# ScalarE's step order in a fused attention and MLP kernel, changed by single moves

## The chip, the cores and the metric

The kernel runs on one core of one Trainium2 chip. The metric is the device time of one execution in microseconds (us): the median of the runs of a kernel. A core has five engines that work side by side, each through its own list of instructions in order: TensorE (PE in the profile, with its weight loads as PEld), VectorE (DVE), ScalarE (ACT), GpSimd (POOL) and SyncE (SP). [...]

## The reference

A polynomial-sketch attention (batch 4, 4 heads, 1088 positions, head size 32, sketch size 8) feeds a wave MLP over the 128 joined channels:

```python
def phi(x):                                   # x: B,H,S,D; S1, S2: 8 x 32
    a = np.einsum('rd,bhsd->bhsr', S1, x)
    b = np.einsum('rd,bhsd->bhsr', S2, x)
    return np.einsum('bhsi,bhsj->bhsij', a, b).reshape(*x.shape[:-1], r * r)
q_p, k_p = phi(q), phi(k)
kv  = np.einsum('bhsf,bhsd->bhfd', k_p, v)
z   = np.sum(k_p, axis=2)
num = np.einsum('bhsf,bhfd->bhsd', q_p, kv)
den = np.einsum('bhsf,bhf->bhs', q_p, z)[..., None] + 1e-06
x = num / den                                  # then (B,H,S,D) -> (B, S, H*D)
theta  = x @ w_theta
zr, zi = x * np.cos(theta), x * np.sin(theta)
y = np.einsum('ts,bsd->btd', w_tok_r, zr) + np.einsum('ts,bsd->btd', w_tok_i, zi)
u = x + y
out = u + np.maximum(u @ w_ch, 0.0)
```

## The kernel before

The inputs come as 64-bit floats. Each 1088-long axis is cut into 9 chunks of 128 partitions, treated in 3 groups of 3 chunks. For each of the 4 batches the kernel makes the key features and the key-value sums (stages `kT`, `kf`, `kv`, `kvb`), the query slices (`qT`), the levels (products of queries with parts of the sums, `levels`), the denominators (`den`), the numerators (`num`), a balancing scale (`even`), and the angle stage (`theta`), which leaves x·cos and x·sin in a tile `z`. The token mixing is then done for pairs of batches by a Strassen-like scheme of products (`m10`, `m12`, `m20`, ...) of `z` with the rows of the two token matrices; sums that the products need are made by transfers that GpSimd issues and that add to their destination (`join`, L348, "accumulating transfers" below).

Everything is written down first as a list of 1147 steps, each an `Op` with its engine (P, V, A, G or S) and a function that issues its instructions. The tables at the head of the file then say how they are issued: `SEQUENCE` is the order of all steps, written out; an engine's own order is the order of its steps in it. `PLACES` deals every temporary tile to a slot of its class. `FILLS` asks for filler matmuls on TensorE: `(n, k)` puts k of them in front of step n, and a negative k puts them into the step's own PSUM tile before its own matmuls. No scheduler reorders anything behind this; the waits follow from the order and the slots. They are made for the built program on counts: an instruction waits for an engine's count of finished steps.

The steps of ScalarE that are spoken of below, by the profile's lines before the change:

- L619 and L621: unpacking of a half row pair of the token matrices that SyncE has loaded as 64-bit words into a `zs` tile. Two L619 turn the high words into floats in a `big` tile (one for each row), one L621 turns the low words into integers in another `big` tile, which VectorE or an accumulating transfer then adds.
- L795: copy of the key features from PSUM. L1036: copy of the levels from PSUM, three to a batch.
- L1141: copies of transposed numerator features from PSUM (the transposes are TensorE's L1137). L1150: copies of the numerators into `xT`.
- L1191: the sum of squares of `xT` (stage `even`). L1077: `xT` times that scale.
- L1094, L1097, L1098, L1100: the angle's rounding, its magnitude, its cosine and its sine; behind them VectorE's product at L334 (`zs<-ps,g`) writes `z`.
- L1359: two copies of a finished product sum out of PSUM into a spare tile (`hf`), which are handed on to later sums by accumulating transfers.

TensorE's product steps all pass through one helper, L354, and VectorE's two-operand steps through L334.

Of the kernel before, what the change touches and what calls it, by code (L numbers as in the profile page):

```python
# [53 lines left out]
    295, 136, 17, 67, 182, 185, 68, 69, 137, 241, 239, 18, 234, 235, 37, 183, 322, 242, 96, 237, 70, 71, 291,  # L54
    293, 296, 210, 72, 73, 74, 89, 90, 33, 159, 323, 310, 211, 212, 213, 75, 80, 187, 81, 306, 307, 186, 308,
    27, 28, 29, 175, 184, 176, 311, 22, 82, 83, 324, 220, 221, 297, 132, 133, 19, 84, 30, 177, 178, 160, 161,
    190, 346, 43, 163, 164, 243, 244, 85, 86, 214, 215, 135, 188, 101, 222, 223, 328, 309, 386, 87, 88, 102, 39,
    347, 350, 91, 92, 93, 169, 170, 240, 44, 97, 98, 103, 23, 410, 191, 45, 162, 112, 312, 113, 99, 313, 245,
    20, 246, 189, 349, 459, 104, 463, 464, 465, 466, 348, 352, 298, 455, 456, 457, 192, 193, 226, 139, 140, 194,
    325, 329, 458, 460, 461, 141, 462, 388, 105, 138, 195, 196, 197, 247, 299, 467, 468, 46, 394, 94, 100, 300,  # L60
    248, 249, 250, 469, 108, 198, 106, 227, 199, 302, 470, 326, 471, 353, 472, 200, 201, 202, 25, 387, 390, 473,
    251, 252, 253, 389, 142, 107, 110, 111, 474, 327, 254, 255, 256, 143, 144, 109, 475, 145, 146, 147, 203,
    204, 261, 413, 165, 301, 205, 206, 207, 303, 208, 338, 257, 258, 259, 171, 172, 47, 148, 149, 150, 351, 411,
    260, 395, 397, 151, 152, 209, 476, 402, 304, 477, 478, 479, 153, 480, 484, 481, 154, 155, 156, 157, 396,
    491, 412, 48, 267, 268, 492, 493, 494, 262, 269, 158, 216, 217, 265, 266, 485, 270, 173, 482, 483, 305, 495,
    124, 400, 125, 487, 488, 263, 271, 272, 486, 118, 405, 404, 499, 501, 114, 166, 179, 450, 496, 489, 273,
    274, 26, 167, 119, 120, 500, 330, 331, 24, 115, 490, 502, 503, 275, 339, 276, 116, 41, 168, 174, 180, 497,
    126, 370, 277, 332, 684, 688, 121, 122, 403, 224, 505, 689, 685, 504, 506, 392, 333, 690, 498, 398, 218,
    127, 128, 401, 283, 692, 693, 181, 694, 695, 42, 40, 686, 687, 691, 264, 696, 373, 228, 229, 282, 314, 697,
    279, 219, 316, 698, 699, 700, 701, 515, 517, 518, 434, 340, 117, 507, 509, 318, 315, 341, 399, 123, 702,  # L70
    129, 130, 362, 286, 284, 703, 525, 319, 451, 519, 520, 508, 225, 230, 231, 232, 317, 372, 704, 334, 524,
    705, 371, 285, 706, 709, 707, 510, 393, 511, 512, 526, 513, 710, 452, 516, 720, 713, 336, 557, 558, 406,
    559, 560, 335, 514, 708, 521, 342, 561, 562, 391, 632, 563, 564, 716, 453, 714, 553, 554, 555, 556, 721,
    722, 723, 354, 724, 715, 337, 717, 436, 522, 531, 711, 344, 712, 278, 345, 565, 566, 435, 357, 365, 454,
    725, 726, 718, 407, 719, 730, 732, 356, 634, 343, 527, 567, 568, 569, 408, 570, 571, 530, 572, 280, 281,
    355, 529, 528, 532, 533, 662, 748, 750, 418, 288, 573, 574, 523, 542, 727, 589, 590, 591, 592, 593, 582,
    585, 586, 583, 584, 733, 734, 320, 409, 594, 595, 587, 588, 575, 576, 577, 728, 747, 376, 426, 578, 579,
    639, 289, 608, 610, 739, 419, 735, 580, 581, 321, 817, 821, 822, 437, 741, 729, 749, 358, 818, 819, 823,
    751, 752, 753, 754, 813, 814, 815, 636, 414, 415, 416, 417, 360, 361, 611, 816, 635, 617, 359, 534, 374,
    375, 820, 364, 736, 755, 764, 763, 440, 377, 742, 731, 363, 537, 539, 756, 429, 366, 367, 738, 740, 737,  # L80
    759, 536, 428, 432, 368, 369, 422, 420, 424, 743, 744, 438, 745, 746, 757, 619, 620, 599, 596, 597, 824,
    825, 826, 633, 601, 421, 378, 541, 612, 621, 613, 602, 827, 828, 829, 830, 831, 607, 598, 603, 832, 623,
    761, 760, 433, 758, 762, 765, 766, 609, 538, 614, 615, 627, 600, 772, 771, 604, 775, 769, 427, 430, 605,
    606, 770, 626, 629, 640, 287, 833, 616, 618, 439, 381, 630, 643, 644, 834, 837, 835, 883, 441, 425, 379,
    382, 383, 442, 443, 446, 423, 380, 384, 385, 637, 645, 641, 774, 838, 431, 638, 622, 624, 625, 628, 631,
    642, 656, 768, 444, 448, 540, 928, 836, 535, 543, 839, 840, 767, 544, 773, 776, 658, 777, 657, 445, 447,
    449, 646, 647, 925, 841, 844, 842, 843, 845, 545, 651, 668, 846, 847, 789, 650, 859, 861, 848, 858, 655,
    788, 667, 654, 666, 549, 653, 862, 661, 863, 864, 865, 660, 786, 546, 669, 652, 648, 778, 659, 779, 860,
    866, 868, 870, 867, 884, 799, 878, 793, 850, 670, 797, 849, 852, 791, 853, 854, 550, 551, 871, 677, 930,
    671, 851, 672, 665, 681, 790, 1028, 680, 926, 798, 682, 1025, 805, 855, 649, 806, 856, 857, 877, 880, 1006,  # L90
    801, 809, 683, 663, 674, 872, 874, 873, 807, 869, 794, 802, 1027, 881, 876, 792, 1010, 1009, 810, 1024, 885,
    800, 808, 796, 875, 879, 882, 1007, 1012, 804, 787, 1008, 795, 803, 1011, 673, 893, 886, 907, 911, 1034,
    664, 910, 888, 1018, 1019, 811, 891, 901, 1026, 676, 1032, 890, 900, 889, 899, 1021, 1014, 1015, 812, 782,
    679, 1029, 1023, 783, 1035, 547, 927, 894, 895, 892, 896, 548, 897, 1047, 1013, 1044, 1016, 1017, 1046,
    1051, 940, 915, 902, 916, 909, 914, 1045, 903, 784, 1020, 934, 935, 1033, 917, 913, 898, 912, 1030, 904,
    918, 905, 678, 944, 675, 906, 924, 919, 1036, 780, 951, 942, 1039, 552, 1040, 1048, 1022, 1058, 945, 952,
    887, 922, 932, 1037, 950, 1049, 908, 929, 1070, 1053, 1054, 1052, 1055, 923, 1050, 1060, 1056, 1059, 936,
    937, 1057, 1061, 955, 943, 946, 1075, 1062, 1071, 1063, 941, 931, 1031, 1065, 1091, 1041, 1064, 1066, 921,
    781, 966, 785, 1092, 1093, 1094, 947, 963, 933, 1067, 938, 1095, 1096, 956, 961, 962, 1042, 1068, 1097,
# [5 lines left out]
    999, 1119, 1112, 1114, 1120, 1113, 1000, 1001, 1121, 1115, 1129, 1124, 1123, 1131, 1137, 1138, 1132, 1142,  # L105
    1139, 1140, 1141, 1144, 1143, 1145, 1146,
)
PLACES = (
    55, 59, 47, 48, 60, 2, 0, 14, 6, 7, 4, 11, 8, 21, 8, 8, 6, 24, 3, 46, 28, 3, 62, 61, 40, 45, 1, 60, 54, 47,
    61, 45, 46, 55, 48, 57, 49, 52, 51, 47, 60, 60, 41, 60, 54, 34, 60, 39, 59, 50, 35, 61, 42, 61, 45, 36, 48,  # L110
    46, 58, 51, 61, 58, 41, 61, 45, 37, 62, 44, 55, 48, 36, 61, 42, 56, 50, 38, 51, 50, 30, 9, 20, 58, 59, 43,
    53, 15, 57, 60, 19, 61, 44, 57, 36, 58, 43, 60, 35, 58, 42, 60, 34, 45, 51, 32, 10, 17, 57, 56, 42, 52, 13,
    58, 57, 60, 40, 55, 34, 55, 43, 58, 35, 57, 39, 62, 36, 31, 49, 29, 5, 12, 59, 62, 44, 52, 14, 58, 49, 48,
    53, 54, 50, 45, 55, 46, 47, 58, 49, 62, 53, 54, 46, 51, 46, 56, 50, 47, 62, 48, 54, 62, 43, 56, 58, 57, 31,
    58, 55, 61, 28, 55, 59, 56, 33, 55, 60, 56, 32, 16, 0, 18, 3, 4, 12, 2, 10, 21, 5, 19, 8, 14, 20, 11, 9, 7,
    22, 7, 24, 9, 23, 21, 23, 8, 26, 9, 23, 15, 26, 13, 23, 15, 25, 1, 24, 7, 22, 5, 26, 11, 25, 11, 26, 13, 24,
    5, 26, 13, 25, 19, 27, 60, 55, 57, 4, 47, 17, 22, 37, 38, 58, 55, 62, 34, 37, 56, 59, 56, 35, 36, 61, 60,
    59, 20, 57, 60, 38, 61, 59, 37, 57, 58, 34, 55, 58, 29, 60, 41, 55, 42, 27, 60, 60, 59, 6, 52, 6, 25, 34,
    37, 57, 59, 57, 34, 38, 59, 57, 56, 38, 37, 59, 56, 61, 11, 61, 56, 35, 39, 57, 61, 38, 42, 57, 61, 37, 40,
    59, 56, 28, 62, 61, 27, 61, 59, 58, 20, 49, 1, 24, 38, 35, 62, 56, 60, 38, 37, 61, 56, 59, 36, 38, 62, 59,  # L120
    62, 6, 56, 61, 36, 41, 57, 56, 34, 44, 57, 60, 35, 40, 60, 62, 30, 58, 39, 55, 44, 55, 60, 27, 60, 62, 59,
    15, 45, 15, 26, 23, 34, 36, 35, 61, 57, 55, 58, 13, 57, 58, 35, 43, 57, 57, 37, 44, 59, 60, 34, 40, 23, 33,
    31, 57, 56, 30, 33, 36, 38, 37, 35, 60, 55, 56, 42, 40, 59, 59, 42, 62, 44, 60, 41, 58, 40, 32, 29, 27, 13,
    58, 59, 61, 43, 40, 62, 59, 43, 58, 41, 62, 39, 62, 41, 62, 39, 62, 44, 61, 57, 55, 58, 43, 59, 39, 62, 58,
# [1578 lines left out]
```

## Time and profile before

| | |
|---|---|
| median of 3 runs | 222.46 us (221.44, 222.64, 222.46) |
| the profiled execution | 222.71 us |
| its span on the core | 220.9 us |
| TensorE's granted clock | 1.00 |
| TensorE busy | 213.4 us of the span |
| VectorE busy | 188.2 us |
| ScalarE busy | 130.9 us in 277 instructions |
| GpSimd | 80.3 us |
| moved by transfers | 48.78 MB |

The span is what the profiler sees between the first and the last instruction of the core; the execution's own time lies 1.81 us above it. Lines are those of the kernel's file, so all TensorE products stand under L354, told apart by their tiles. An idle time in brackets before a row, such as `[0.59 <-ACT hf L1359]`, is the time that the engine stood and the instruction that released it.

### The profile page before, as it was taken

The page shows a single profiled execution, that of the slowest core. Times are in us where ns is not written, and L with a number is a line of the kernel's source. Part 1 is how long each engine was busy: PE and PEld are TensorE (multiplying, and loading weights), DVE is VectorE, ACT ScalarE, POOL GpSimd, SP SyncE. Part 2 cuts the span into 40 slices and gives each one's busy share as a digit, 9 for nine tenths or more (in the row PEclk, how much of TensorE's full clock was granted, in tenths as well). Part 3 has the DMA queues.
Part 4 walks back from the last instruction along what each step waited for, and adds up shares of the span by engine and source line. Part 5 has one row for each costly group of instructions (what it writes and reads, how often), then busy time and mean ns, then how long its engine had stood idle before and what let it go on. Part 6 is the DMA issues. An engine that isn't in the chain of part 4 may idle for free.

```text
span 220.9 us, 4195 instructions
## 1 busy us (share of the span) xinstructions
PE 213.4 (97%) x1481; PEld 178.4 (81%) x1481; DVE 188.2 (85%) x449; ACT 130.9 (59%) x277; POOL 80.3 (36%) x119
## 2 busy tenths in 40 slices
PE   7999999999999999898999999999999999999993
PEld 4798988987898886767888887888788888888782
DVE  1698999999999999898999999699999966876452
ACT  3989789799999999889999721864030200000000
POOL 1159960001031141425163367891062829060000
PEclk9999999999999999999999999999999999999999
DMA  6999999999988989699999999999953979677332
GB/s 192 414 415 409 372 346 331 418 387 394 277 295 161 260 311 250 145 239 202 262 167 176 276 179 183 190 180 188 181 87 47 164 116 143 100 107 110 58 49 51
DMA packets 34969, 48.78 MB, mean 221 GB/s; under 512 B 19204, under 2 KB 22276, under 8 KB 34820
## 3 DMA queue, kind: packets, MB, share of 16 engines
q0 software_dynamic: 10368, 18.21, 47.0%
q1 hardware_dynamic: 24580, 30.30, 41.5%
q8 instruction: 12, 0.20, 0.3%
q14 instruction: 9, 0.07, 0.1%
HBM read 28.07 MB, written 2.23 MB: 137 GB/s over the span
## 4 chain that ended last, share of the span: by engine, by line
PE 62%; DVE 18%; ACT 8%; DMA 7%; issue 2%; POOL 0%; ACTq 0%; DVEq 0%; POOLq 0%
PE ps L354 57%; DMA big<-big 7%; DVE big L334 3%; DVE g L334 3%; DVE sm L341 2%; PE ps L388 2%; PE ps L1003 2%; DVE sm L334 2%; DVE hf L338 1%; ACT big L619 1%; DVE lv L334 1%; DVE big L338 1%; PE ps L1085 1%; DVE sm L338 1%; ACT big L621 1%
## 5 line engine op out<-in xcount | busy, mean ns | idle before, releaser
L354 PE MATMUL ps<-big,zs 128*128 128x288 f32 (+3 forms) x450 | 105.6, 385 | 1.2 <-ACT hf L1359 0.6
L354 PEld LDWEIGHTS ps<-big,zs 128*128 128x128 f32 x450 | 81.4, 190 | 18.0 <-ACT lv L1036 0.9
L348 POOL DMA_DIRECT2D big<-big x49 | 47.3, 1265 | 79.2 <-DVE big L338 21.6
L341 DVE SCALAR_TENSOR_TENSOR big<-ps,even,big 128x272 f32<-128x272 f32 (+3 forms) x34 | 16.0, 487 | 10.0 <-PE ps L354 9.9
L619 ACT ACTIVATE big<-zs 128x544 f32<-128x544 f32 x32 | 22.1, 710 | 2.8 <-DMA zs<-w_tok 1.5
L621 ACT ACTIVATE big<-zs 128x1088 int32<-128x1088 uint32 x16 | 19.5, 1228 | 1.9 <-DMA zs<-w_tok 1.1
L348 POOL DMA_DIRECT2D big<-g x10 | 11.9, 1326 | 11.4 <-ACT g L1560 5.9
L354 PE MATMUL ps<-mf,big 128*128 128x96 f32 x72 | 14.4, 295 | 0.1
L348 POOL DMA_DIRECT2D big<-hf x9 | 10.2, 1159 | 11.6 <-ACT hf L1359 7.8
L1328 ACT COPY g<-ps 128x128 f32<-128x128 f32 x2 | 0.5, 266 | 23.1 <-PE ps L1326 23.1
L338 DVE TENSOR_SCALAR big<-big 128x544 int32<-128x544 int32 (+1 forms) x33 | 14.0, 449 | 0.0
L354 PEld LDWEIGHTS <-hf 128*128 128x128 f16 (+1 forms) x144 | 12.1, 106 | 1.9 <-issue 0.6
L334 DVE TENSOR_TENSOR zs<-ps,g 128x768 f32<-128x768 f32 (+2 forms) x20 | 12.5, 627 | 0.9 <-ACT g L1100 0.9
L354 PE MATMUL ps<-big,big 128*128 128x128 f32 x72 | 11.6, 281 | 0.3 <-DMA big<-hf 0.3
L334 DVE TENSOR_TENSOR g<-lv 128x768 f32<-128x768 f32 x12 | 11.0, 953 | 0.9 <-PE ps L1137 0.8
L334 DVE CUSTOM_DVE_ANT_0 big<-big,big 128x1088 uint16<-128x1088 uint16 x16 | 11.5, 721 | 0.2
L354 PE MATMUL ps<-mv,hf 128*128 128x96 f16 x108 | 11.1, 206 | 0.3 <-DVE mv L909 0.2
L354 PEld LDWEIGHTS ps<-mf,big 128*128 128x128 f32 x72 | 10.9, 191 | 0.5 <-issue 0.4
L334 DVE TENSOR_TENSOR big<-big,hf 128x1152 f32<-128x1152 f32 x8 | 10.8, 1366 | 0.0
L354 PE MATMUL ps<-w,big 128*128 128x128 f32 x76 | 10.7, 278 | 0.0
L354 PEld LDWEIGHTS ps<-w,big 128*128 128x128 f32 x76 | 9.7, 192 | 0.9 <-ACT big L1150 0.6
L341 DVE SCALAR_TENSOR_TENSOR big<-ps,big 128x288 f32<-128x288 f32 (+1 forms) x15 | 6.6, 440 | 4.2 <-PE ps L354 3.9
(215 smaller groups left out, 439.0 us busy)
## 6 DMA issues: line engine op xcount, KB each, us to landing
zs<-w_tok SPq DMA_DIRECT2D x17, 1088.0 KB, 11.2
big<-big POOLq DMA_DIRECT2D x40, 272.0 KB, 5.6
big<-k_l SPq DMA_DIRECT2D x7, 576.0 KB, 6.8
big<-q_l SPq DMA_DIRECT2D x4, 576.0 KB, 8.3
big<-v_l SPq DMA_DIRECT2D x4, 576.0 KB, 6.7
big<-hf POOLq DMA_DIRECT2D x3, 576.0 KB, 9.6
big<-hf POOLq DMA_DIRECT2D x6, 272.0 KB, 8.6
big<-g POOLq DMA_DIRECT2D x10, 136.0 KB, 4.1
```

Of the source, the lines that this page charges most:

```text
L334: eng.tensor_tensor(out=o, in0=a, in1=b, op=f)
L338: (eng or V).tensor_scalar(out=o, in0=a, scalar1=s1, scalar2=s2, op0=op0, **kw)
L341: (eng or V).scalar_tensor_tensor(out=o, in0=a, scalar=s, in1=b, op0=op0, op1=op1)
L348: op("G", n * 2.55e-3, lambda: G.dma_start(dst(), src(), accum_op=ALU.add), w, r, kind=2)
L354: T.matmul(o, lhs, rhs, start=start, stop=stop, skip_group_check=True)
L388: T.matmul(nowhere() if out is None else out, idle()[:, 0:P], idle(), start=True, stop=True, skip_group_check=True)
L619: op("A", 0.19 + HT * 0.0009, lambda j=j: A.activation(dst[j](), words()[1][:, j * HT:(j + 1) * HT].bitcast(F32), AF.Prelu, scale=scale, a ...
L621: op("A", 0.22 + S * 0.0009, lambda: A.activation(stp().rearrange("p r n -> p (r n)"), words()[0].bitcast(U32), AF.Copy, scale=2.0**-29), ...
L1003: T.transpose(tr()[:, i * P:(i + 1) * P], x()[:, g * GC + i].rearrange("p h d -> p (h d)"), ident())
L1085: T.transpose(x()[:, i], xs()[:, off + i * P:off + (i + 1) * P], ident())
L1328: op("A", act(P), lambda: A.copy(ot()[:, :P], tp()), [ot], [tp])
```

## The change

Only the three tables at the head of the file differ. TensorE, VectorE, GpSimd and SyncE keep each its own order of steps: 421, 343, 84 and 51 of them. Of ScalarE's 248 steps the first eleven stay, and behind them steps are moved singly, some by one or two places, others by ten and more. All temporary tiles are dealt again to slots, so that some steps of other engines wait for other earlier users of a slot than before. `FILLS` gets one entry: one more filler matmul, in the PSUM tile of step 177, a key feature product of batch 2.

The stretch of the order that holds ScalarE's steps around 82 to 105 us, before and after, cut out of the tables:

```diff
@@ SEQUENCE
...
-    722, 723, 354, 724, 715, 337, 717, 436, 522, 531, 711, 344, 712, 278, 345, 565, 566, 435, 357, 365, 454,
-    725, 726, 718, 407, 719, 730, 732, 356, 634, 343, 527, 567, 568, 569, 408, 570, 571, 530, 572, 280, 281,
-    355, 529, 528, 532, 533, 662, 748, 750, 418, 288, 573, 574, 523, 542, 727, 589, 590, 591, 592, 593, 582,
-    585, 586, 583, 584, 733, 734, 320, 409, 594, 595, 587, 588, 575, 576, 577, 728, 747, 376, 426, 578, 579,
-    639, 289, 608, 610, 739, 419, 735, 580, 581, 321, 817, 821, 822, 437, 741, 729, 749, 358, 818, 819, 823,
-    751, 752, 753, 754, 813, 814, 815, 636, 414, 415, 416, 417, 360, 361, 611, 816, 635, 617, 359, 534, 374,
-    375, 820, 364, 736, 755, 764, 763, 440, 377, 742, 731, 363, 537, 539, 756, 429, 366, 367, 738, 740, 737,
...
+    556, 721, 722, 723, 724, 354, 715, 337, 522, 436, 531, 711, 712, 344, 278, 345, 435, 565, 566, 454, 725,
+    726, 718, 719, 407, 730, 732, 634, 343, 527, 365, 567, 727, 357, 568, 569, 408, 570, 571, 530, 572, 280,
+    281, 529, 528, 533, 532, 662, 748, 750, 355, 356, 418, 288, 573, 574, 523, 542, 589, 590, 591, 592, 593,
+    582, 585, 586, 583, 584, 733, 734, 320, 409, 594, 587, 588, 575, 576, 577, 728, 738, 376, 426, 578, 579,
+    639, 289, 595, 608, 610, 739, 580, 321, 817, 821, 822, 747, 581, 749, 735, 358, 818, 819, 823, 729, 751,
+    752, 754, 753, 813, 814, 815, 636, 414, 415, 416, 417, 360, 820, 361, 437, 611, 635, 617, 359, 534, 824,
+    420, 374, 375, 755, 764, 763, 440, 377, 741, 742, 731, 537, 539, 756, 363, 366, 736, 367, 740, 737, 759,
...
@@ PLACES
...
@@ FILLS
-    (290, 1), (64, 14),
+    (290, 1), (64, 14), (177, -1),
```

In this stretch 355 and 356 are a pair of L619 and 357 their L621; 365 and 437 are L621 of other rows, 419 an L619; 532 and 533 are the L1359 pair and 542 the TensorE product that goes on in the PSUM that they copy; 727 is the L1191 of batch 2; 732, 741 and 750 are L1094; 752, 753 and 754 are L1097, L1098 and L1100 of one group, and 755 is VectorE's product behind them; 588, 595 and 581 are L1150; 738, 747 and 729 are L1077; 816, 820 and 824 (this last earlier than in the order before) are the L1036 of batch 3; 764 is the TensorE product `m12` that needs 755. Among the other moves that the prediction speaks of, 178 is the feature copy L795 of batch 2, which goes from behind 177 to a place behind the L795 steps of batch 0, and 512 is the L1098 ahead of VectorE's 514.

116 rows, old and new, of tables (PLACES, SEQUENCE) are left out of this document.

## The prediction

> **What bounds the kernel now.** I read the page first, for the share of each engine.
>
> ```profile
> PE 213.4 (97%) x1481; PEld 178.4 (81%) x1481; DVE 188.2 (85%) x449; ACT 130.9 (59%) x277; POOL 80.3 (36%) x119
> ```
>
> TensorE (PE) is busy for 97% of the span, so a change of ScalarE's order can only pay through the idle left on TensorE, or through an engine that sets TensorE's pace. So the second view is busy time by stretches, in columns start:end, length, then PE, PEld, DVE, ACT, POOL, clock, DMA share and GB/s.
>
> ```profile
> 31.00:93.00 62.00, 60.80 (x575) 52.38 (x574) 60.73 (x131) 57.72 (x123) 9.48 (x12) 1.00 0.95 295
> 93.00:104.30 11.30, 10.73 (x94) 8.11 (x92) 9.45 (x23) 10.19 (x23) 4.74 (x6) 1.00 1.07 230
> ...
> 130.00:160.00 30.00, 30.00 (x201) 24.29 (x200) 26.87 (x61) 11.53 (x24) 15.77 (x18) 1.00 1.08 185
> ```
>
> Between 31 and 104 us TensorE, VectorE (DVE) and, to 93, the transfers are all almost full, and ScalarE (ACT) is 57.72 of 62. Only in 93 to 104.3 does VectorE drop, to 9.45 of 11.3. From 130 to 160 TensorE is busy without a gap and the transfers are full (a share over 1 counts packets that overlap). The third view, the waits of VectorE from 31 to 104.3, says what that drop is:
>
> ```profile
> DVE zs L334 <- ACT g L1100: 0.9, 1, 0.9
> DVE g L334 <- PE ps L1137: 0.8, 1, 0.8
> ```
>
> Two waits and no others. The fourth view, the chain that ended last (start, length, what), shows what stands in front of the longer one:
>
> ```profile
> 80.51 8.77 DMA big<-big
> 89.36 0.66 ACT big L619
> ...
> 92.05 7.72 DMA big<-big
> ...
> 154.61 61.76 PE ps L354 x286
> ```
>
> A transfer ends at 89.28 and frees ScalarE's row step L619; behind it stand the two copies L1359; behind these another transfer, L621, the sine L1100, VectorE's product L334, and the TensorE product that starts at 104.29. From there the chain holds TensorE's rows alone, of which the last begins at 154.61. So the time before is set by when TensorE reaches 104.29, and what is gained in front of it is kept as far as no later wait eats it.
>
> **The change part by part.** The order view shows TensorE, VectorE, GpSimd and SyncE with the same steps in the same order; ScalarE's 248 steps are moved from the twelfth on; buffers are dealt again; one filler matmul is added. The sum goes against the profiled execution, 222.71 us (span 220.9, 1.81 around it); the median of the three runs, 222.46, is 0.25 below, and I shift the result by that.
>
> *First wait, 87 to 92 us.* The timeline of ScalarE and that of TensorE, with the idle before a row in brackets (the rows from 95 on are for the step after the next):
>
> ```profile
> 84.58 2.38 ACT L621 ACTIVATE big<-zs 128x1088 int32<-128x1088 uint32 x2
> ...
> 87.52 0.57 ACT L1094 ACTIVATE g<-ps 128x384 f32<-128x384 f32 x1
> 89.36 1.30 ACT L619 ACTIVATE big<-zs 128x544 f32<-128x544 f32 x2 [1.28 <-DMA big<-big]
> 90.57 0.65 ACT L1359 COPY hf<-ps 128x288 f32<-128x288 f32 x2
> ...
> 91.49 1.17 ACT L1191 ACTIVATE big<-big 128x1152 f32<-128x1152 f32 x1
> ...
> 95.23 0.48 ACT L1150 COPY big<-ps 128x384 f32<-128x384 f32 x1 [0.16 <-PE ps L354]
> ...
> 99.85 1.22 ACT L621 ACTIVATE big<-zs 128x1088 int32<-128x1088 uint32 x1 [0.87 <-DMA big<-big]
> 100.97 0.48 ACT L1094 ACTIVATE g<-ps 128x384 f32<-128x384 f32 x1
> ...
> 106.95 0.61 ACT L1077 ACTIVATE g<-big,even 128x384 f32<-128x384 f32 x1
> ```
>
> ```profile
> 84.59 0.94 PE L354 MATMUL ps<-w,big 128*128 128x128 f32 x6
> ```
>
> ```profile
> 91.00 1.18 PE L354 MATMUL ps<-big,zs 128*128 128x288 f32 x4 [0.59 <-ACT hf L1359]
> 92.02 1.70 PE L1137 MATMUL ps<-ident,g 128*128 128x128 f32 x12
> ...
> 104.29 2.07 PE L354 MATMUL ps<-big,zs 128*128 128x288 f32 x8 [0.57 <-DVE zs L334]
> ```
>
> In the new order the two L621 of 84.58 go behind the L1094 of 87.52, the square L1191 goes between them, and the L1359 pair comes next, ahead of the two L619 that wait for the transfer. Without the L621 in front, the L1094 can start about 2 us sooner, at 85.5, when its six matmuls of 84.59 end. From its end at 86.1 come an L621 (2.38 for two rows that overlap by 0.1, so 1.13 each), the L1191 (1.07), an L621 of 1.13 and the pair (0.65): done at about 90.1 instead of 91.22. TensorE's product at 91.00 then starts when TensorE is free. By the bracket that is 0.59 earlier; but start to start a row here gives way sooner than its end says (91.00 + 1.18 = 92.18 against the next start 92.02, 0.16 overlap), so I take 0.59 + 0.16 = 0.75. [...] By the end times alone this term would be 0.59, by starts it is 0.75.
>
> *VectorE at 93.75.* Its timeline at the two waits:
>
> ```profile
> 93.75 0.96 DVE L334 TENSOR_TENSOR g<-lv 128x768 f32<-128x768 f32 x1 [0.80 <-PE ps L1137]
> ...
> 103.45 0.69 DVE L334 TENSOR_TENSOR zs<-ps,g 128x512 f32<-128x512 f32 x1 [0.89 <-ACT g L1100]
> ```
>
> It waits 0.80 for the transposes L1137, which follow that product and the L1141 copies. Both come 0.75 earlier, ScalarE because the L1191 now lies in front. The wait shrinks to 0.05, and VectorE runs 0.75 early, free for its next waited step at 103.45 - 0.89 - 0.75 = 101.8.
>
> *VectorE at 103.45.* The copy at 95.23 waits for TensorE and so starts at 94.48. Between it and VectorE's release the new order drops an L619 (half of 1.30, 0.60 after an overlap of 0.1), the L1094 of 100.97 (0.38) and the 0.87 of waiting for the transfer, and adds the L1077 of 106.95 (0.51), another L1150 (0.38) and a level copy L1036 (like an L1150 but wider; estimated at 0.45): -0.51. The sines themselves are then done two steps sooner, but in the built program VectorE's wait rests on a count that also takes in the L621 behind them, so I count to its end: 103.45 - 0.75 - 0.51 = 102.19, **-1.26**. TensorE's product at 104.29 follows by the same amount: its own idle of 0.57 + 0.16, with the 0.75, leaves room for 1.48 (0.16 again the overlap). It also needs the third L1036 copy of its levels, which the new order puts directly behind that L621, ready near 102.7, in front of 103.0.
>
> *The early steps.* Moves before 84 us can only cost, as VectorE and TensorE have nothing to gain there. One timeline row or two of ScalarE, TensorE and VectorE:
>
> ```profile
> 22.28 0.34 ACT L795 COPY big<-ps 128x192 f32<-128x192 f32 x1
> ...
> 76.55 0.62 ACT L1098 ACTIVATE g<-g,halfpi 128x384 f32<-128x384 f32 x1
> ```
>
> ```profile
> 28.00 0.44 PE L354 MATMUL ps<-mv,hf 128*128 128x96 f16 x2 [0.21 <-DVE mv L909]
> ```
>
> ```profile
> 78.04 0.95 DVE L334 TENSOR_TENSOR zs<-ps,g 128x768 f32<-128x768 f32 x1
> ```
>
> The feature copy at 22.28 goes some twelve steps back, to about 26.9, and a feature product that TensorE did ahead of 28.00 then waits about half a microsecond for it. The filler, one more matmul just before, adds about 0.3 if it is like one of the four at 91.00 (1.18). TensorE waits 0.21 at 28.00 anyway, for VectorE, so 0 to 0.6 of this can pass on; VectorE not being late at that place, I take 0. At 78.04 VectorE needs the cosine L1098 of 76.55; laid one after another with their row lengths, ScalarE's new steps end it at 77.9 instead of 77.17, so its slack falls from 0.87 to about 0.1. Estimated cost of the places where slack falls below 0.2: 0.1, range 0 to 0.4.
>
> *The transfers.* Row loads move because their tiles come free at other times (the new order moves several unpacking steps L619 and L621 by 2 to 9 us), but the queue is full to 93 us (DMA share 0.95), so I cost them at nothing; if that cover is gone, a late load costs its lateness at the L619 that reads it. Late in the kernel most accumulating transfers are released by TensorE's products, so they move with it; but at the DMA share of 1.08 from 130 to 160 they queue, and where a product starts right as its tile lands, an unmoved landing takes the gain back. I take 0.1 lost; the range is 0 to 1.0, the difference between the two long landings of the chain (8.77 and 7.72).
>
> The sum: -1.26 + 0.1 + 0.1 = -1.06; 222.71 gives 221.65, the median 222.46 gives **221.4 us**.
>
> **The rivals.** What this kernel's measurement can tell from no change is about 0.5%, 1.11 us, so faster means under 221.35 and slower over 223.57.
>
> *Larger gain.* If VectorE's step at 103.45 isn't held by the L621, or ScalarE arrives sooner, both waits go whole: 0.80 + 0.89 = 1.69, and with nothing lost later, 220.8. For it: the sines alone would be done near 99.8. Against: the count, and that the late losses must be zero.
>
> *Part of the gain.* Only the 0.75 is kept and 0.2 is lost: 221.9. The mechanism is the transfer of 92.05 to 99.77, for which the L621 of 99.85 waits. A row load issued behind the two L619 of 89.36 now goes out over a microsecond later, beside that transfer. If it pushes the landing from 99.77 to over 101.5, the L621 starts no sooner than in the sum plus 0.7. Against it: the transfer itself is issued behind the L1359 copies, which come 1.1 us earlier, so it can also land sooner. For it: the transfer of 80.51 took 8.77, longer than this one's 7.72, so landings move by a microsecond from one place to another. [...]
>
> *Slower.* ScalarE has only 4.3 us of idle in 31 to 93, and a moved step that has to wait stops all behind it. If waits at new places make it late, the first to pay is VectorE at 78.04, with its 0.1 of slack: beyond a cosine that ends at 78.0 each microsecond costs one, until the gain is gone at 79.2; from 80.4 the kernel is over 223.6. That takes 2.4 us of new waiting between 31 and 78: more than half of all its idle there, and I put it at 224.2.
>
> *The change doing nothing* would need both waits to come back at other places; it lies in the second rival.
>
> **How the numbers follow.** The forecast (0.6 to 1.5 gained) gets 0.46, with somewhat more than half, 0.26, past the bound, as the two losses are estimates that may be nil; the larger gain 0.16; part of the gain 0.20; slower 0.18. That gives faster 0.42, same 0.40, slower 0.18. The range goes from 220.4 (the larger gain, 220.8, with the runs' own scatter below it) to 223.8, which leaves out the worse part of the slower case. The forecast's own range is 221.0 to 221.9.
>
> **What would show it.** Right: ScalarE shows no wait above 0.3 for a transfer before its L1359 pair, TensorE's idle of 0.59 is gone, VectorE waits less than 0.1 where it waited 0.80, and TensorE's chain of products starts near 103.0. Wrong: new waits of VectorE or TensorE for ScalarE between 20 and 80 us, a landing for the L621 later than 101, or a wait of TensorE for a transfer between 130 and 160, each with its length.

## The result: slower by 0.84%, and the profile after

The changed kernel takes 1.0084 times the kernel before, with a 95% interval of 1.0055 to 1.0113 (11 runs each); on a second occasion, beside other kernels, 1.0095 (1.0055 to 1.0134). That is 1.9 to 2.1 us more. The forecast was 221.4 us, 1.1 us less; its range ended at 223.8, and 222.46 times 1.0084 is 224.3.

In some executions of either kernel the mean granted clock of TensorE is 0.97 (in the two that were traced, both of the changed kernel, it is 0.50 for 13.7 us from 21 or 22 us on), which the ratios here and below leave out but for one of h5's six. The profile below is of the second occasion, an execution at clock 1.00 (223.83 us, span 222.0).

Page, windows and VectorE's waits from 31 to 104.3 us, as they were shown of before:

```profile
PE 214.0 (96%) x1482; PEld 178.4 (80%) x1482; DVE 188.7 (85%) x449; ACT 131.9 (59%) x277; POOL 81.9 (37%) x119
```

```profile
31.00:93.00 62.00, 60.56 (x574) 52.22 (x571) 60.78 (x131) 57.23 (x119) 12.36 (x16) 1.00 0.94 294
93.00:104.30 11.30, 11.30 (x100) 8.79 (x99) 9.52 (x24) 10.48 (x22) 3.77 (x5) 1.00 1.06 231
130.00:160.00 30.00, 29.44 (x195) 23.32 (x194) 28.12 (x64) 12.21 (x26) 17.55 (x20) 1.00 1.07 182
```

```profile
DVE g L334 <- PE ps L1137: 1.2, 1, 1.2
DVE zs L334 <- ACT big L621: 0.3, 1, 0.3
```

VectorE's second wait has shrunk from 0.9 to 0.3 and now ends with the L621, as forecast, but the first has grown from 0.8 to 1.2 instead of vanishing. TensorE has 0.56 of idle between 130 and 160 where it had none. The chain that ended last says why:

```profile
81.00 10.53 DMA big<-big
91.53 0.14 issue
91.67 1.16 PE ps L354 x4
...
147.73 11.97 DMA big<-big
159.74 57.71 PE ps L354 x268
```

The transfer that landed at 89.28 now lands at 91.53, 10.53 us after its issue instead of 8.77. What follows it is no longer ScalarE but TensorE's product m20 itself. Much later a transfer stands in the chain again, right in front of the product m30 at 159.74. TensorE's and ScalarE's timelines of the changed kernel:

```profile
91.67 1.16 PE L354 MATMUL ps<-big,zs 128*128 128x288 f32 x4 [1.23 <-DMA big<-big]
...
158.26 1.18 PE L354 MATMUL ps<-big,zs 128*128 128x288 f32 x4 [0.26 <-DMA big<-big]
159.74 2.56 PE L354 MATMUL ps<-big,zs 128*128 128x288 f32 x10 [0.30 <-DMA big<-big]
```

```profile
85.59 0.49 ACT L1094 ACTIVATE g<-ps 128x384 f32<-128x384 f32 x1 [0.29 <-PE ps L354]
...
89.37 0.68 ACT L1359 COPY hf<-ps 128x256 f32<-128x256 f32 x2
```

The ScalarE row is as forecast: the L1094 starts at 85.59 (85.5 was said) and the L1359 pair is done at 90.05 (90.1 was said). It just didn't help: TensorE then waits 1.23 for the transfer.

### The profile page after: what moved, and what is told of

Read it like the earlier page. It is cut to its first block, busy times and chain, and to the rows that moved or that the text cites. A ratio compares the mean times of both kernels' runs of the same rounds, so it can differ in the third digit from the quotient of the medians.

```text
span 227.1 us, 4198 instructions
## 1 busy us (share of the span) xinstructions
PE 219.4 (97%) x1482; PEld 183.8 (81%) x1482; DVE 189.2 (83%) x449; ACT 132.0 (58%) x277; POOL 78.8 (35%) x119
## 4 chain that ended last, share of the span: by engine, by line
PE 58%; DMA 17%; ACT 10%; DVE 7%; issue 3%; POOL 3%; SPq 0%; POOLq 0%
PE ps L354 53%; DMA big<-big 15%; POOL big L348 3%; DMA big<-k_l 2%; ACT big L619 2%; PE ps L780 2%; ACT big L621 2%; DVE g L334 2%; DVE sm L341 1%; PE ps L1003 1%; PE ps L1137 1%; DVE sm L334 1%; PE ps L1085 1%; DVE hf L338 1%; ACT g L1141 1%
## 5 line engine op out<-in xcount | busy, mean ns | idle before, releaser
L348 POOL DMA_DIRECT2D big<-big x49 | 47.7, 1338 | 89.1 <-PE ps L780 26.6
L619 ACT ACTIVATE big<-zs 128x544 f32<-128x544 f32 x32 | 22.0, 714 | 2.8 <-DMA zs<-w_tok 2.8
L621 ACT ACTIVATE big<-zs 128x1088 int32<-128x1088 uint32 x16 | 19.7, 1232 | 0.0
L354 PE MATMUL ps<-mf,big 128*128 128x96 f32 x72 | 15.3, 309 | 0.1
L354 PEld LDWEIGHTS <-hf 128*128 128x128 f16 (+1 forms) x144 | 13.1, 114 | 1.7 <-DVE hf L338 0.8
L334 DVE TENSOR_TENSOR zs<-ps,g 128x768 f32<-128x768 f32 (+2 forms) x20 | 12.5, 627 | 0.4 <-PE ps L354 0.3
L354 PE MATMUL ps<-sbk,g 128*128 128x64 f32 x72 | 12.3, 324 | 0.1
L354 PEld LDWEIGHTS ps<-sbk,g 128*128 128x128 f32 x72 | 11.7, 244 | 0.5 <-issue 0.5
L354 PEld LDWEIGHTS ps<-mf,big 128*128 128x128 f32 x72 | 11.6, 203 | 0.4 <-issue 0.4
L334 DVE CUSTOM_DVE_ANT_0 big<-big,big 128x1088 uint16<-128x1088 uint16 x16 | 11.5, 720 | 0.2
L334 DVE TENSOR_TENSOR g<-lv 128x768 f32<-128x768 f32 x12 | 11.0, 950 | 0.6 <-PE ps L1137 0.5
L334 DVE TENSOR_TENSOR big<-big,hf 128x1152 f32<-128x1152 f32 x8 | 10.8, 1366 | 0.0
```

The source lines that it names most:

```text
L334: eng.tensor_tensor(out=o, in0=a, in1=b, op=f)
L348: op("G", n * 2.55e-3, lambda: G.dma_start(dst(), src(), accum_op=ALU.add), w, r, kind=2)
L354: T.matmul(o, lhs, rhs, start=start, stop=stop, skip_group_check=True)
L619: op("A", 0.19 + HT * 0.0009, lambda j=j: A.activation(dst[j](), words()[1][:, j * HT:(j + 1) * HT].bitcast(F32), AF.Prelu, scale=scale, a ...
L621: op("A", 0.22 + S * 0.0009, lambda: A.activation(stp().rearrange("p r n -> p (r n)"), words()[0].bitcast(U32), AF.Copy, scale=2.0**-29), ...
```

## The experiments

The theories: **A**, the gain near 90 to 104 us is real and the loss comes from elsewhere; **B**, the gain is given back by transfers later; **D**, the loss comes from unpacking steps that let row loads out later, so that the transfer in front of m20 lands later; **E**, it comes from the other moves; **Q**, the queue of accumulating transfers and TensorE's row of products are two chains of nearly one length that meet at m30. All ratios are to the kernel before.

**The changed kernel once more** (no edit).

> The changed kernel once more, unaltered, for a profile at full clock. Theory A (the forecast's gain between 87 and 104 us is real, and the loss lies elsewhere): TensorE's product m12 comes 1.2 to 1.4 us sooner after the transposes L1137 than in the kernel before, counted from 80 us, and more than that is lost before 80 us or after 130 us. Rival B (no gain there): m12 keeps its distance of before, and the whole loss is there. Time expected 223 to 224 at clock 1.00, 229 if the clock is halved for some 13 us near 20 to 34 us.

228.72 us, and the kernel before 227.59 on the same occasion, one execution of each. That pair decides nothing and is used no further.

**New order only from 83 us on, and only up to 83 us.**

```diff
  ScalarE's steps
- before: the old order throughout
+ h1: old order through step 436, then the rest in the new order; old FILLS
+ h2: new order through step 436, then the rest in the old order; new FILLS
+ h5: old order through 436, new order through 816, then old again; old FILLS
  (PLACES dealt anew for each)
```

> ScalarE in the order of before up to the L619 of 83 us, in the new order behind it; no filler; tiles dealt to fit. Theory A (the gain near 87 to 104 us is real and is kept to the end, the loss of the change comes from before 83 us): 1.0 to 1.3 us faster than before, about 0.5%. Rival B (the gain is real but is given back by transfers between 120 and 160 us, where products wait for accumulated tiles): within 0.4 us of before, with waits of TensorE for a transfer near 158 us. Rival C (no gain at all there): 0 or slower, m12 not earlier than 104.

> The reverse: ScalarE in the new order up to 83 us, with the filler, and in the order of before behind it. Theory A: 1.5 to 3 us slower than before (the change's 1.9 plus what its late part gained). Rival B: 1.5 to 2 us slower, as the change itself, since its late part is then worth nothing. Rival D (the early part costs only by runs in which TensorE's clock is halved near 20 to 34 us): as before in runs at clock 1.00, 5 us more in the others.

> ScalarE in the new order from 83 us to the last level copy L1036 of batch 3 only, before and behind that in the order of before; no filler. Theory A: 1.0 to 1.3 us faster than before. Rival B (given back by the new order's late part, behind 118 us): 1.0 to 1.3 faster as well, while the kernel that is new from 83 us on is not; if B means the accumulating transfers in general, then both are as before. Rival C: no gain in either.

Measured: h1 1.0129 (1.0075 to 1.0182), h2 1.0187 (1.0139 to 1.0235), h5 1.0102 (1.0040 to 1.0165). All three are slower, so neither A nor B came out as expected, and h2's own rival D (another D than in the list above: a loss only with the clock halved) fails, as h2 loses 4.2 us with a granted clock of 0.99 or more in every execution. But h1 and h5 do not test what they were meant to test. h1's chain:

```profile
80.69 9.18 DMA big<-big
89.89 0.35 ACT big L621
90.23 0.76 issue
90.99 0.66 ACT hf L1359 x2
```

An L621 starts right as the transfer lands: in the new deal of tiles its output tile took the slot that this transfer frees, a wait that the changed kernel doesn't have. The same happens in h5, at 89.81. h2 is free of that, and its profile shows TensorE waiting 3.1 us for the L1359 pair, which there stands behind L619 again, and the transfer landing at 91.35. So the early half moves that landing by 2 us on its own (it is 89.86 and 89.78 in h1 and h5, which have the old early half), and the old order behind it pays in full.

**One swap: the two copies first.**

```diff
-    725, 726, 718, 407, 719, 730, 732, 356, 634, 343, 527, 567, 568, 569, 408, 570, 571, 530, 572, 280, 281,
-    355, 529, 528, 532, 533, 662, 748, 750, ...
+    725, 726, 718, 407, 719, 730, 732, 634, 343, 527, 567, 568, 569, 408, 570, 571, 530, 572, 280, 281, 529,
+    528, 532, 533, 356, 355, 662, 748, 750, ...
```

> The kernel before with one move: ScalarE's two copies L1359 in front of the two row steps L619 that wait for the transfer landing at 89.3 us. Same tiles, no filler. This is the forecast's first term alone. Forecast's theory: TensorE's product m20 starts 0.6 to 0.75 us sooner, and the kernel is 0.3 to 0.75 us faster. Rival D (the transfer engines are what binds between 60 and 160 us, and m20 itself reads the tile which that transfer completes): m20 follows the landing by 0.1 us whatever ScalarE does; the row load behind the two L619 goes out a little later, and the time is as before within 0.3 us.

Measured 0.9999 (0.9968 to 1.0030). m20 starts at 90.15 instead of 91.00, 0.85 sooner, so the forecast's first term is there. In the trace nothing is left of it at 104:

```profile
100.43 1.23 ACT L621 ACTIVATE big<-zs 128x1088 int32<-128x1088 uint32 x1 [1.67 <-DMA big<-big]
```

```profile
104.05 0.69 DVE L334 TENSOR_TENSOR zs<-ps,g 128x512 f32<-128x512 f32 x1 [1.72 <-ACT g L1100]
```

ScalarE's L621 waits 1.67 for the next accumulating transfer where it waited 0.87, and VectorE 1.72 where it waited 0.89. That transfer landed at 100.35 instead of 99.77, although it was issued 1.6 us sooner. The row load that had gone out 1.36 us ahead of it, at 90.69, now goes out 0.60 behind it, at 91.05, and lands 2.84 later; that the load beside it is what holds the transfer up is an inference from these times. The traced execution took 223.72 us, 1.8 more than the median of this kernel (221.95), so the median execution need not lose as much there. The rival's price of nothing fits, but the interval also holds most of the gain that the forecast's theory had given (0.3 to 0.75 us, 0.13 to 0.34%), so the time doesn't decide between them. The rival's reason (m20 bound by the landing) is not found at this place: the transfer landed at 89.63, half a microsecond before m20.

**The unpacking steps alone, and all the others alone.**

```diff
  ScalarE's steps
- before: the old order throughout
+ r: L619, L621 and the other unpacking steps where the new order has them, the rest in the old order; old FILLS
+ x: the unpacking steps where the old order has them, the rest in the new order; new FILLS
```

> The kernel before with ScalarE's unpacking steps of loads alone (L619, L621, and those of the last row and of w2) at the places that they have in the changed kernel, all other ScalarE steps in the order of before, no filler. Rival D: the change's loss is here, since the loads' tiles come free 1 to 5 us later and the transfers fall behind: 1.3 to 2.5 us slower than before, with the transfer in front of m20 landing 0.6 us or more later. Rival E (the loss comes from the other moves, such as the feature copy that TensorE waits for near 26 us): within 0.4 us of before.

> The complement: all ScalarE steps but the unpacking ones at their places of the changed kernel, with the filler, the unpacking steps at their places of before. Rival D: within 0.5 us of before, loads as in the kernel before. Rival E: 1 to 2 us slower, with TensorE late from 26 us on.

Measured: r 1.0126 (1.0075 to 1.0177), x 1.0066 (1.0032 to 1.0101). In r the transfer in front of m20 lands at 93.1, 3.8 us later than before, and m20 starts at 93.21. That is D. But x isn't free either: its 1.5 us are what E had said of it, although the transfer lands at 88.11 there. The two add up to more than the whole change, as half of an order laid into half of another makes waits of its own (in x VectorE waits 1.0 us for L1098 and TensorE 0.8 for a small copy L821, neither of which the changed kernel shows). So this pair does not divide the loss.

**Three steps put back.** In the changed kernel the L621 numbered 341, which lets go of the load tile of rows 2, comes 9 us later, and the two unpacking steps of the last row, 451 and 452, 1 and 8 us sooner. The loads take the freed tiles in turn, so the loads of 71.2 and 79.1 us hang on these. The tiles were dealt to fit: in f1 20 of the 441 lie in other slots than in the changed kernel.

```diff
  ScalarE's steps, against the changed kernel
-    ..., 517, 509, 452, 451, 372, ..., 513, 512, 130, 560, 232, 341, 564, 717, ...
+    ..., 517, 509, 341, 451, 372, ..., 513, 512, 452, 130, 560, 232, 564, 717, ...
```

> The changed kernel with three of ScalarE's steps back at their places of before: the L621 of 69.9 us (rows 2, second half-set) and the two unpacking steps of the last row, 71.7 and 77.9 us. They are what lets the row loads of 71.2 and 79.1 us go out. Rival D (late loads in front of the transfer that m20 reads are the main loss): those two loads go out at 71 and 79 as before, that transfer lands within 0.7 us of 89.3, and the kernel is 1 to 2 us faster than the changed one, 221.5 to 222.5. Rival E (the loss is in the other moves): no faster than the changed kernel, 223.5 or more.

> The kernel with only the unpacking steps moved, with the same three steps left at their places of before. Rival D: of its 2.8 us over before, 1.5 or more go away. Rival E: the loss stays at 2 us or more, since other unpacking steps in ScalarE's way cause it.

Measured: f1 1.0009 (0.9965 to 1.0054): the change's whole 0.84 to 0.95% is gone. The 20 other slots changed with it and were not tried alone. r2 1.0072 (1.0026 to 1.0118): 0.54% of r's 1.26 gone, 1.2 us, between what D and E had said, and with intervals that overlap; what is left says that other moved unpacking steps cost something where the rest of the order isn't made for them. SyncE's issues of the loads, in the kernel before, the changed one and f1:

```profile
71.18 0.38 SPq L614 DMA_DIRECT2D zs<-w_tok  x1
...
76.13 3.33 SPq L614 DMA_DIRECT2D zs<-w_tok  x2
```

```profile
71.73 3.94 SPq L614 DMA_DIRECT2D zs<-w_tok  x2
...
80.28 0.37 SPq L614 DMA_DIRECT2D zs<-w_tok  x1
```

```profile
70.78 5.04 SPq L614 DMA_DIRECT2D zs<-w_tok  x2
...
79.07 0.37 SPq L614 DMA_DIRECT2D zs<-w_tok  x1
```

The first of the three loads goes out 0.55 later in the changed kernel, the last at 80.28 instead of 79.1; in f1 both are back. ScalarE's rows show what they waited for. In the kernel before, 341 and 452 (L644) are

```profile
69.93 1.23 ACT L621 ACTIVATE big<-zs 128x1088 int32<-128x1088 uint32 x1
...
77.85 1.22 ACT L644 ACTIVATE big<-zs 128x1088 int32<-128x1088 uint32 x1
```

and in the changed kernel 451 (L641) and 341 are

```profile
70.50 1.20 ACT L641 ACTIVATE big<-zs 128x1088 f32<-128x1088 f32 x1
...
79.00 1.25 ACT L621 ACTIVATE big<-zs 128x1088 int32<-128x1088 uint32 x1
```

These end at 71.16 and 79.07, and at 71.70 and 80.25: each of these loads goes out 0.03 us or less after the end of one of the three steps. The same split shows over all traces in which TensorE's clock is whole up to there: with the three steps moved (the changed kernel, h2, r and q2 below) the transfer in front of m20 lands at 91.35 to 93.07, with them in their old places (before, h1, h5, m1, x, f1, r2 and g1 below) at 87.88 to 90.84. What it does to the transfers, in windows of the kernel before, the changed one and f1 (last two columns DMA share and GB/s):

```profile
80.00:89.00 9.00, 9.00 (x57) 6.61 (x57) 8.83 (x20) 7.83 (x15) 3.16 (x3) 1.00 1.05 280
89.00:92.00 3.00, 2.41 (x16) 1.96 (x15) 2.96 (x6) 2.64 (x6) 0.49 (x1) 1.00 0.34 52
```

```profile
80.00:89.00 9.00, 9.00 (x57) 6.60 (x57) 8.86 (x20) 8.65 (x17) 2.80 (x3) 1.00 0.94 243
89.00:92.00 3.00, 1.77 (x14) 1.49 (x13) 2.92 (x7) 2.55 (x6) 1.66 (x4) 1.00 0.79 146
```

```profile
80.00:89.00 9.00, 9.00 (x61) 6.67 (x60) 8.84 (x19) 8.15 (x17) 2.71 (x3) 1.00 1.04 261
89.00:92.00 3.00, 3.00 (x22) 2.69 (x21) 2.95 (x6) 3.00 (x6) 1.26 (x3) 1.00 0.11 20
```

The engines that are full before (1.05) and in f1 (1.04) stand part of the time in the changed kernel (0.94), and they move more between 89 and 92 us (a share of 0.79 instead of 0.34), while TensorE's busy time there falls from 2.41 to 1.77. In f1 it is 3.00: the transfer lands at 89.1, and m20 starts at 90.68. From there to 104 us f1 is near the forecast:

```profile
93.24 0.96 DVE L334 TENSOR_TENSOR g<-lv 128x768 f32<-128x768 f32 x1 [0.29 <-PE ps L1137]
...
102.33 0.69 DVE L334 TENSOR_TENSOR zs<-ps,g 128x512 f32<-128x512 f32 x1 [0.29 <-PE ps L354]
```

VectorE's step comes at 102.33 (102.2 was said) and m12 at 103.08, 1.21 sooner than before (1.26 was said). But the kernel is no faster. TensorE's timeline and the chain of f1:

```profile
158.14 3.04 PE L354 MATMUL ps<-big,zs 128*128 128x288 f32 x12 [0.26 <-DMA big<-big]
```

```profile
146.47 11.62 DMA big<-big
158.10 0.04 issue
158.14 55.48 PE ps L354 x248
```

At m30 TensorE waits for an accumulated tile again. From m30 to the end of the span is a fixed length (222.0 - 159.74 = 62.3 in the changed kernel, 220.6 - 158.14 = 62.5 in f1), so the time is set by when m30 may start: the later of TensorE and of the queue. In the kernel before (220.9 - 158.67 = 62.2) the two meet: the tile for m30 landed at 158.62, and m30 is the row

```profile
158.67 0.51 PE L354 MATMUL ps<-big,zs 128*128 128x288 f32 x1
```

with no idle in front of it that the profile shows.

**Two transfers taken out of the queue**, first from the kernel before and from the changed one, then from f1:

```diff
         for b, h in ((p, 1), (q, 0), (q, 1)):
             at("carry", b, "_", h)
+            if (b, h) in ((1, 0), (2, 1)):
+                op("G", HT * 2.55e-3, lambda: None, cells(xT[b], h * HT, (h + 1) * HT), [us[b]], kind=2)
+                continue
             join(...)
```

> The kernel before without two of its accumulating transfers of 272 KB (the spare sum isn't added to the first half of batch 1 and the second half of batch 2; that part of the output is another sum). They lie in the full queue between 142 and 156 us, some 1.35 us each. Theory Q (TensorE's row of products and the queue of accumulating transfers are two chains of nearly the same length that meet at the product of 158.7 us): no change within 0.5 us, as TensorE has no idle behind 104 us. Rival: the queue alone sets the time, 2 us faster.

> The changed kernel without the same two accumulating transfers (the same part of the output is another sum). Theory Q: the changed kernel is behind because this queue ends late, and TensorE waits for it: 1 to 2 us faster than the changed kernel, 222 to 222.7, about what the kernel before takes without the two. Rival E (TensorE itself is late from its early steps on): no change, 223.3 or more.

> The changed kernel with the three steps back, and without the two accumulating transfers of the earlier pair of runs (that part of the output is another sum). Its m12 came 1.2 us sooner and its m30 0.5 sooner, as the queue's last tile landed only 0.5 sooner. Theory Q: with 2.7 us taken from the queue, TensorE's 1.2 are kept to the end: 0.8 to 1.2 us faster than before, 0.6 or more faster than the same kernel with all transfers. Rival: no faster than before within 0.3 us, so the 1.2 us were lost for another reason.

Measured: q1 0.9998 (0.9952 to 1.0044), q2 1.0019 (0.9983 to 1.0054), g1 0.9961 (0.9927 to 0.9994). These kernels leave two transfers out, so part of their output is another sum. The times agree with Q in all three. The kernel before gains nothing within 0.5%, and TensorE is busy without a gap up to m30 anyway; that the queue alone sets the time, with 2 us to be gained, is excluded. The changed kernel gets most of its loss back, 0.65% or 1.4 us. f1, whose m12 comes 1.2 us sooner, is now 0.39% faster than before, 0.9 us, which is the size of the forecast's gain. How it got there is not seen: f1's and g1's intervals overlap and are of two occasions, and the traced execution of g1 took 223.36 us, 1.8 more than its median of 221.53. In it m12 starts at 102.73, 1.56 sooner than before, and the tile for m30 lands at 157.29, so the queue holds nothing up; but TensorE waits 1.00 for VectorE at 136.69, and m30 starts only at 159.14.

**The three steps alone, in the kernel before.**

```diff
  ScalarE's steps, against the kernel before
-    ..., 509, 315, 341, 130, 319, 451, 519, ..., 710, 452, 560, 708, 521, ...
+    ..., 509, 315, 452, 451, 130, 319, 519, ..., 710, 560, 341, 708, 521, ...
```

> The kernel before with those three unpacking steps alone moved to their places of the changed kernel (in two places of the list), tiles dealt to fit, no filler. If they are sufficient for the loss: the two loads go out 0.6 and 1 us later, the transfer in front of m20 lands 1.5 us or more later, and the kernel is 1.5 to 2.8 us slower than before. If they only hurt together with the other moves: within 0.5 us of before.

Measured 1.0085 (1.0046 to 1.0123), as much as the whole change. In its profile the loads go out at 73.76 and 83.54 instead of 71.18 and 79.10, but a part comes another way:

```profile
PE ps L1085 <- ACT sm L821: 2.0, 1, 2.0
```

TensorE waits 2.0 for a small copy L821 that now stands behind the two unpacking steps. In the changed kernel that copy has been moved as well, and TensorE does not wait for it. The traced execution took 226.58 us, 2.5 more than the median of this kernel, and TensorE's granted clock in it is 0.50 from 75.3 to 78.7 us, so it shows more lateness than the median can hold. The three are thus enough for a loss of this size, but which share of it comes by the late loads stays open here.

**The changed kernel beside these.**

> The changed kernel itself beside these two on one chip, for its profile at full clock: 1.5 to 2.2 us slower than before at clock 1.00. The transfer that m20 reads lands near 91.9 instead of 89.3 us, m20 follows it within 0.2 us, m12 comes within 0.5 us of the kernel before, and the tile for the product m30 lands 1 to 2 us later than before, with TensorE waiting for it.

Its ratio and profile are those of the first section. The landing at 91.53, m20 at 91.67, m12 at 104.17 (104.29 before) and the two waits of 0.26 and 0.30 at m30's tiles all came as written; the tile for m30 landed at 159.7, 1.1 later than before.

## Why the prediction was wrong, step by step

*The bound.* "The time before is set by when TensorE reaches 104.29." That reading of the chain is what failed first. The chain shows one path, and TensorE's rows without idle hid a second one beside it: the queue of accumulating transfers, whose tile for m30 lands at 158.62, right as m30 may start at 158.67. q1 (no gain with a shorter queue) and f1 (no gain with an m12 that comes 1.2 us sooner) fit two chains of one length; g1, with both, is faster by 0.39%, with an interval that ends at 0.06%.

*First wait.* ScalarE's part was right to 0.1 us. "TensorE's product at 91.00 then starts when TensorE is free" was not: m20 also reads the tile that the transfer completes. At 89.28 that wait was hidden behind ScalarE's, and at 91.53 it is the one that ends last. The term was -0.75 and measured +0.67 in the changed kernel (91.67 against 91.00), -0.32 in f1 and -0.85 in m1.

*VectorE at 103.45.* Right in size: -1.26 was said, f1 shows -1.21 at m12. The changed kernel keeps only 0.12 of it, having lost 0.67 at m20. The wait on the L621, which the prediction put down to a count, also has a reason in the slots: the new z tile takes the slot of the load that this L621 reads last. A wait on that slot ends with the L621 as well, so the sum is the same.

*The early steps.* Right in the main: the feature copy holds TensorE, by 0.30 where half a microsecond was said, and none of it is left on VectorE by 44 us (a step `g` of L334 starts at 44.06, and at 44.14 before). VectorE did not wait at 78.04, so the slower rival's mechanism did not occur.

*The transfers.* This is the step that turned the sign. Loads that go out late were costed "at nothing" since the queue is full to 93 us (a share of 0.95). That is a mean over 62 us. In the same trace, right where the first of these loads goes out, the share is 0.31:

```profile
70.00:72.00 2.00, 2.00 (x23) 1.62 (x20) 2.00 (x5) 2.00 (x5) 0.00 (x0) 1.00 0.31 54
```

With two loads in it, from 80 to 89 us, it is 1.05, and from 89 to 92, when these have landed, 0.34. In the changed kernel the share is 0.94 in place of 1.05 from 80 to 89 us, the transfer that m20 reads lands 2.25 us later, and the term put at nothing is what turned the -0.75 of the first wait into +0.67; with the three steps back, in f1, the lateness is gone. The second rival had a late load beside a transfer, but at the next one and with a price that only lowered the gain; that next transfer landed at 97.92, 1.85 us sooner than before.

*The late loss.* 0.1 was taken, with a range of 0 to 1.0. In f1 0.68 of the 1.21 is lost by m30 (158.14 against 158.67 leaves 0.53), and the ratio is 1.0009. That a product may start "right as its tile lands" was in the prediction; its 0.1 was too small, and 0.68 lies in its range.

What stays open is whether f1 keeps the 0.5 us that it still has at m30 (its interval, 0.9965 to 1.0054, holds both that and nothing), what the 20 other slots of f1 do, and the path of g1's gain. No version in these runs that computes the whole output beats the kernel before.

## What to carry to other kernels

When an engine seems busy to the end, look for what lands just as it is needed: a second chain of the same length takes a gain of the first, and a loss in either is passed on (here the tile that landed at 158.62 for a product at 158.67). Before a wait is moved out of the way, list all that its successor reads, not only the engine that released it last. A step that frees a load's tile is part of the transfer's schedule (here the loads of 71.18 and 79.10 went out within 0.03 us of the end of such a step), and a reordering that looks only at compute engines will move it by accident. A share that is a mean over 62 us (0.95 here) does not say that the queue is full at a given place (0.31 from 70 to 72 us): look at the two microseconds in which the moved transfer goes out.

## What the runs showed of the hardware that was not expected

In the kernel before, the transfers that add to their destination moved far less than plain loads at the same share of the engines: 185 GB/s at a share of 1.08 from 130 to 160 us, when nearly only they ran, against 280 at 1.05 from 80 to 89 us, when two loads were among them. Within these 9 us the accumulating transfers moved 1.01 MB for a share of 58.5%, the loads 1.48 MB for 45.3%. And issuing such a transfer sooner did not make it land sooner: in the kernel with the one swap it went out 1.6 us earlier and landed 0.6 later, with a load issued 0.6 us behind it that landed 0.5 us before it.

In the trace with the three steps alone, TensorE was idle for 1.96 us up to 73.94, and its granted clock was 0.50 from 75.3 to 78.7 us. That the wait brought on the lower clock is not shown.
